# Gathered columns for eight of nine V units, own PSUM tiles for the last pair, and a new order for every engine

## The chip, the cores and the metric

The kernel runs on one core of a Trainium2 chip. The metric is the time of one execution in microseconds of the device; lower is better. Besides TensorE (PE in the profile; its weight loads are PEld), the core has VectorE (DVE), ScalarE (ACT), GpSimd (POOL) and SyncE (SP). SP does no arithmetic here: it issues DMAs in its own order, and ACT issues some too.

## The reference

One transformer block with conditioning, for 2048 positions of 448 features, in bf16:

```
mod = silu(c) @ w_mod, cut into sa, ca, ga, sb, cb, gb
h = layernorm(x) * (1 + ca) + sa
x = x + ga * (attention(h) @ wo)
h = layernorm(x) * (1 + cb) + sb
x = x + gb * (silu(h @ w1) @ w2)
```

The attention has 16 heads of 28 features. Each position looks at 8 keys: itself and the positions 2, 4, ... 14 behind it. w1 is 448 x 1792, w2 is 1792 x 448.

## The kernel before

**Layout.** Even and odd positions never meet in the attention, so each half is a sequence of 1024 positions with a plain window of 8. The kernel holds h transposed (features on partitions) in `hT`, two tiles `hA` and `hB` of 512 positions per parity. The sequence is worked in four chunks of 256 positions per parity for normalisation and projection, in nine attention units of two blocks (57 queries and 64 keys per block and parity), and in four chunks for the feed-forward part.

**Stages and the names of their operations.** A number after the name is the chunk, unit or pair.

- `ldx`, `ldm`, `ldwv`, `ldwqk`, `ldwo`, `ldw1`, `ldw2`, `ldc`: loads. `pad`: four copies that spread the QK weights into `wp` (L441).
- `n1m.*` and `n2m.*`: layer norms of 256 rows: statistics (`st` on DVE, L361 and L362, or `mean`, `sq` with ACT, L371), `rstd` on POOL (L374, L375), `nm`, `xn0`, `xn1` (L393 on ACT, L395 on DVE).
- `h0x.trp` on PE for the first chunk, or `n1m.tr`, a DMA transpose issued by SP (L412). Then `hk.mod`: scale and shift per feature, on DVE (L236) or ACT (L234).
- `qkkg.S` and `.C`: the QK projection of chunk k, head group g (L483), and `.ev`, its copy out of PSUM (L487).
- `vu.S` and `.C`: V for the keys of unit u (L517 or L518) and `.ev` (L523).
- `lgu`: logits of a unit (L555), `exu0`, `exu1`: exp on ACT (L562), `mku`: mask on DVE (L613), `avu`: attention times V on PE (L629), `rcu` and `onu`: normalise on DVE (L636, L641), `otru`: DMA transpose by SP (L644), `alu`: copies that close the gaps (L651 to L659).
- `wom.S` and `.C`: output projection of 256 rows (L686), `resm`: residual with row sums on DVE (L694).
- `gk.mod`, `f1ki.S`, `.C` (L714), `.ev` (silu on ACT, L719); `f2m.S0` to `.C2` (L741) for row pairs 0 to 6, and `f27.F0` to `.F3` (L753) for the last pair; `yam`: add the residual on DVE (L774), `stom`: store (L779, L781).

Matmuls with 64 rows of contraction come in twos on the two halves of the array: `.S` uses the half with the same number as the PSUM bank, `.C` the other one.

**V, apart or whole.** A unit's two key blocks overlap, and each block has an even and an odd half that lie in different places of `hT`. For a unit in `APART` the weights are loaded straight from there, in 64 columns for one half at a time: 28 matmuls of 64x64. For any other unit `project_v` first gathers the columns into a tile `hv` with two to four copies (`hvu`, L507) on DVE or ACT, and then takes 128 columns at a time: 14 matmuls of 64x128. Two `hv` tiles are there. Before, only unit 4 is whole.

**PSUM.** Four tiles of two banks. An operation that opens a matmul group takes a tile, and the operation that reads it last gives it back. In the last pair, all four parts (`F0`, `F1`: the even rows; `F2`, `F3`: the two halves of the columns of the odd rows) write one tile, and three adds (`ya70`, `ya71`, `ya72`) read it.

**The order.** `Plan.emit` writes the instructions in the order of the text `ORDER`: a number is an operation (in the order of `P.op` calls), the letter is its engine (p PE, a ACT, v DVE, g POOL, s SP). Each engine runs its own operations strictly in that order; a DMA issue stands in the order of the engine that issues it. A dependency becomes a semaphore wait. `junk` operations are matmuls without use if they are on PE and nothing if they are on SP.

Parts of the queues before, by name:

```
PE   ccol warm junk x6 mod1.mm h00.trp h01.trp v0.S v1.S v0.C v1.C qk03.S qk02.S qk03.C qk02.C qk01.S qk00.S qk01.C qk00.C
     qk11.S qk10.S lg0 qk10.C qk11.C qk13.S qk12.S lg1 qk13.C qk12.C v3.S av0 v3.C v2.S av1 v2.C mod2.mm ga.mm qk20.S lg2 ...
     wo0.C qk32.C v5.S av3 v5.C wo1.S ... av4 v6.S v7.S v6.C v7.C ... v8.S av5 v8.C ... f106.C av6 f104.C ... f20.S2 av7 av8 f20.C0
     ... f26.C2 read f27.F0 f27.F1 f27.F2 f27.F3
DVE  ... n12.st0 n12.st1 mod1.ev h00.mod0 h01.mod0 h01.mod1 pad0 ... ya5 ya4 flag ya6 ya70 ya71 ya72
SP   ldx0a ldx0b ldm_a1 ldx1 ldm_a0 ldwv0 ldwqk0 n13.tr n12.tr ldm_b0 ldm_c0 ldm_c1 ldm_b1 n14.tr ldwo1 n15.tr ...
     otr3 ldw1a0 n20.tr otr4 n21.tr ldw1b1 otr5 ... sto1 sto5 sto70 sto71 sto6
ACT  ldc tab silu_c scT n10.xn0 ldwv1 ... h00.mod1 ldx2 ldx3 ... f136.ev sto72
```

Of the kernel before, what the change touches and what calls it, by code (L numbers as in the profile page):

```python
# [45 lines left out]
32g 241a 16a 242a 132p 129p 193v 192v 194g 130a 133v 137p 235p 138p 134p 167s 17s 168s 172a 243v 244p 236v 237v 238s 18s 195g 169a 139a 245v 171v 170v
135p 144p 140p 136a 200g 145v 246v 201v 185v 141v 202v 203v 173p 196a 197a 253p 254a 255a 176p 146v 256v 174p 177p 186p 175a 247s 266p 178a 248v 147v
267a 187p 257p 205s 268a 204s 258v 259v 21a 179p 260s 182p 180p 206v 208v 239a 188a 209v 207v 183p 249p 216p 184v 269v 181a 279p 280a 281a 250p 251v
252v 261a 217p 218v 189p 318g 319a 20s 270p 190p 262p 213p 263p 214p 320a 321g 271v 282v 272v 191a 273s 264v 265v 283p 222p 322g 325v 225p 19s 215a
326a 327a 328g 329g 223p 226p 224a 210p 284v 323v 324v 285v 292p 227a 211p 274v 293a 294a 275p 219p 330v 331v 212a 276p 332s 295v 278v 286s 277v 401v  # L50
228p 296p 287a 229p 333s 22s 23a 230a 220p 221a 297v 298v 337v 288p 142p 403a 143a 305p 306a 307a 336v 334v 335v 289p 291v 356p 290v 308v 350p 353p
357p 402a 309p 149v 310v 358a 351p 404g 354p 352a 338p 347p 299s 300v 311v 408v 24s 154v 148v 151v 341p 409a 410a 339p 342p 348p 355a 340a 312s 301p
411g 343a 349a 150v 152v 153v 344p 302p 405g 345p 303v 304v 406v 367p 313a 346a 314p 412g 413v 414v 375p 315p 317v 316v 368p 369p 376a 377a 378v 407v
388p 389a 390a 391v 416s 359p 360p 361p 379p 392p 465g 458g 459a 466a 362p 363p 364p 467a 460a 380v 393v 381v 415s 468g 469v 470v 417a 370p 461g 394v
420v 418v 462v 419v 463a 471a 464a 371p 372p 382s 430p 424p 383a 365v 373v 427p 431p 395s 425p 432a 426a 428p 429a 421p 384p 433p 472s 473s 477a 385p
396v 387v 386v 515v 476v 434p 435a 397p 422p 436p 439p 398p 423a 475a 474a 437p 400v 399v 522v 438a 524a 490p 440p 491p 441a 442p 481p 443p 450p 451p
444p 482p 517a 516a 523a 525g 526g 527v 492a 528a 493p 518g 483a 452p 478p 519v 494p 495a 520v 521v 529s 530s 533v 366s 445p 446p 447p 496p 479p 480a
448v 453p 454p 484p 455p 556v 534a 531a 485p 487p 532a 456v 497p 488p 486a 498a 535p 538p 536p 489a 537a 539p 540a 541p 507p 508p 509p 542p 543a 449s
499p 547p 510p 511p 550p 512p 513v 500p 551p 552a 548p 544p 553p 501p 457s 549a 545p 546a 502p 554p 557p 559p 560p 555a 561p 503p 504p 505v 506s 558v
374s 514s 562p 563p 564p 567p 568p 569p 570p 571p 565v 572v 573s 574v 575s 566s 576v 577a  # L60
"""


# [78 lines left out]
def layer(ctx, tc, io, safe):  # L142

    A_x, A_wqkv, A_wo, B_w1, B_w2, c, w_mod, out = io
    nc = tc.nc
# [578 lines left out]
    def ffn2(k):  # L724
        f2_read[k] = []
        for i in range(2):
            m = 2 * k + i
            last_pair = m == 7

            cell = {}  # L730
# [15 lines left out]
                    cell["last"] = x  # L746
            mms = {}
            if last_pair:
                def full(o, par, i0, i1, c0, c1, i=i, cell=cell):
                    t = ps[cell["first"]["slot"]["ps"][0]]  # L750
                    for ii in range(i0, i1):
                        for jj in range(2):
                            matmul(t[:, par, c0:c1], lhsT=hid[:, k % 2, jj, ii, 128 * (2 * i + par):128 * (2 * i + par) + 128], rhs=w2[:, ii + 7 * jj, c0:c1],  # L753
                                   start=(ii == 0 and jj == 0), stop=(ii == 6 and jj == 1))
# [16 lines left out]
            def add(o, m=m, cell=cell, par=None, c0=0, c1=D):  # L771
                t = cell["t"] = outl if m == 7 else outb[o["slot"]["out"][0]]
                p = slice(0, 2) if par is None else slice(par, par + 1)
                V.tensor_tensor(out=t[:, p, c0:c1], in0=ps[cell["first"]["slot"]["ps"][0]][:, p, c0:c1], in1=x_all[:, 2 * m + p.start:2 * m + p.stop, c0:c1], op=ALU.add)  # L774
# [149 lines left out]
```

## Time and profile before

| | us |
|---|---|
| time, median of 3 runs | 170.31 (169.68 to 170.35) |
| the profiled execution | 169.34 |
| its span, first to last instruction | 167.5 |
| PE busy | 156.1 (93%) |
| ACT busy | 102.0 (61%) |
| DVE busy | 86.1 (51%) |
| POOL busy | 25.5 (15%) |
| mean granted clock of TensorE | 0.992 |

The profile is of one execution. The busy time of an engine is that of its instructions without waits, branches and DMA issues; a group of rows gives the source line, the engine, the operation, what it writes and reads, the shape and the count, then busy time and the mean of one, then the idle time ahead of them and what ended it. In the timeline each row is a start, a length, the engine (with q: a DMA issue), the line, the operation and the count of instructions merged. Merged matmuls are pipelined, so a row can reach past the start of the next.

### The profile page before, as it was taken

The numbers are of one execution on the slowest core, as the hardware profiler recorded it, in microseconds if no ns is written. First come the engines' busy times: TensorE is split into PE (matmuls) and PEld (weight loads), VectorE is DVE, ScalarE is ACT, GpSimd is POOL, SyncE is SP. The second block draws the span as 40 slices with busy tenths as digits, with TensorE's granted clock in tenths as the row PEclk, the third lists the DMA queues.
The fourth block names the chain that finished last, engine by engine and source line by source line (L and its number), as shares of the span: only waits on it lengthen the run. The fifth ranks groups of instructions, "written<-read, shape, count | busy, mean of one in ns | idle before, by whom it ended". The sixth has DMA issues, their size and how long they took to land. (4 is left out here: it accounts for less than half of the span.)

```text
span 167.5 us, 6069 instructions
## 1 busy us (share of the span) xinstructions
PE 156.1 (93%) x2670; PEld 80.5 (48%) x2670; DVE 86.1 (51%) x192; ACT 102.0 (61%) x138; POOL 25.5 (15%) x66
## 2 busy tenths in 40 slices
PE   2979979999999999999999999999999999999950
PEld 1254535655455555444556444454444444445540
DVE  3897899987888747692668713302152002002220
ACT  4368657879866869997976695894266620440000
POOL 7460730700002200312034000022000000000000
PEclk9999999999999999999999999999999999999996
DMA  5989978658640999920220950002411000000412
GB/s 138 348 293 242 247 289 135 180 101 171 162 126 21 198 174 293 250 56 7 59 66 22 121 125 4 0 0 57 126 55 55 4 0 4 0 0 4 170 32 87
DMA packets 33453, 18.52 MB, mean 111 GB/s; under 512 B 25102, under 2 KB 33422, under 8 KB 33422
## 3 DMA queue, kind: packets, MB, share of 16 engines
q1 hardware_dynamic: 30208, 14.46, 37.6%
q10 hardware_dynamic: 3214, 3.61, 6.9%
q8 instruction: 23, 0.38, 0.9%
q14 instruction: 8, 0.07, 0.1%
HBM read 10.21 MB, written 1.84 MB: 72 GB/s over the span
## 5 line engine op out<-in xcount | busy, mean ns | idle before, releaser
L719 ACT ACTIVATE both<-ps 128x1024 bf16<-128x1024 f32 x28 | 27.8, 1021 | 23.6 <-PE ps L714 23.6
L741 PE MATMUL ps<-w,both 64*128 64x448 bf16 x392 | 39.9, 349 | 0.0
L714 PEld LDWEIGHTS <-w 64*128 64x128 bf16 x392 | 19.0, 94 | 21.9
L741 PEld LDWEIGHTS <-both 64*128 64x128 bf16 x392 | 18.8, 94 | 18.2
L714 PE MATMUL ps<-wqk,w 64*128 64x512 bf16 x196 | 23.3, 376 | 0.0
L714 PE MATMUL ps<-h,w 64*128 64x512 bf16 x196 | 23.1, 376 | 0.0
L562 ACT ACTIVATE p<-ps 128x912 bf16<-128x912 f32 x18 | 15.8, 928 | 5.7 <-PE ps L555 5.6
L483 PEld LDWEIGHTS <-wp 64*128 64x128 bf16 x224 | 11.0, 94 | 13.4 <-issue 3.2
L694 DVE SCALAR_TENSOR_TENSOR x_all<-ps,x_all 128x448 bf16<-128x448 f32 x16 | 9.3, 621 | 15.0 <-PE ps L686 15.0
L483 PE MATMUL ps<-ha,wp 64*128 64x512 bf16 x112 | 13.2, 377 | 1.1 <-DVE ha L236 1.1
L483 PE MATMUL ps<-hb,wp 64*128 64x512 bf16 x112 | 14.0, 377 | 0.0
L487 ACT CAST qk<-ps 128x1024 bf16<-128x1024 f32 x11 | 11.0, 1016 | 4.0 <-PE ps L483 4.0
L374 POOL TENSOR_SCALAR rs<-mv 128x2 f32<-128x2 f32 x16 | 3.9, 242 | 61.3 <-ACT scr L371 45.6
L393 ACT ACTIVATE xn<-x_all,nm,rs 128x512 bf16<-128x512 bf16 x12 | 9.1, 806 | 6.2 <-DVE nm L381 5.7
L613 DVE TENSOR_TENSOR p<-p,maskb 128x1824 bf16<-128x1824 bf16 x9 | 10.1, 1118 | 4.4 <-ACT p L562 4.4
L774 DVE TENSOR_TENSOR wqk<-ps,x_all 128x896 bf16<-128x896 f32 x4 | 4.4, 1089 | 15.5 <-PE ps L741 13.4
L375 POOL TENSOR_TENSOR rs<-rs,negh 128x2 f32<-128x2 f32 x16 | 11.8, 740 | 1.3
L774 DVE TENSOR_TENSOR ot<-ps,x_all 128x896 bf16<-128x896 f32 x3 | 3.3, 1091 | 16.1 <-PE ps L741 16.1
L361 DVE BATCH_NORM_STATS2 st<-x_all 128x6 f32<-128x448 bf16 x16 | 9.7, 605 | 3.3 <-DMA x_all<-in_A_x_dram 3.3
L395 DVE TENSOR_SCALAR xn<-x_all,mv,rs 128x512 bf16<-128x512 bf16 x20 | 7.3, 402 | 6.9 <-POOL rs L375 6.5
L371 ACT ACTIVATE scr<-x_all,mv 128x448 bf16<-128x448 bf16 x16 | 10.6, 665 | 0.1
L641 DVE TENSOR_TENSOR o<-ps,rc 121x896 bf16<-121x896 f32 x9 | 9.7, 1078 | 0.2
(96 smaller groups left out, 170.8 us busy)
## 6 DMA issues: line engine op xcount, KB each, us to landing
both<-in_w_mod_dram SPq DMA_DIRECT2D x3, 672.0 KB, 6.0
w<-in_B_w_dram SPq DMA_DIRECT2D x3, 448.0 KB, 4.4
x_all<-in_A_x_dram ACTq DMA_DIRECT2D x2, 448.0 KB, 4.7
out_dram<-wqk SPq DMA_DIRECT2D x4, 224.0 KB, 2.0
w<-in_B_w_dram ACTq DMA_DIRECT2D x1, 784.0 KB, 6.1
w<-in_B_w_dram SPq DMA_DIRECT2D x1, 784.0 KB, 5.7
both<-in_w_mod_dram SPq DMA_DIRECT2D x3, 224.0 KB, 5.1
wo<-in_A_wo_dram ACTq DMA_DIRECT2D x1, 672.0 KB, 5.0
```

The lines of the kernel that those rows point to most:

```text
L361: V.bn_stats(out=st[:], in_=x_all[:, us[t], :])
L371: S.activation(out=scr[:, t, :], in_=x_all[:, us[t], :], func=ACTF.Square, bias=mv[:, t, 0:1], accum_out=mv[:, t, 1:2])
L375: G.tensor_tensor(out=rs[:], in0=rs[:], in1=negh[:], op=ALU.pow)
L483: return [matmul(t[:, j, :], lhsT=w, rhs=hT[k // 2][rows, :, kt, CP * (k % 2):CP * (k % 2) + CP], start=start, stop=stop)]
L487: copy_on(o)(out=qk[:, :, g, :, s0:s0 + CP], in_=t[:].rearrange("p j (t s) -> p j t s", t=2))
L562: S.activation(out=p_of[u][:, 2 * t * w:2 * t * w + 2 * w].rearrange("p (j n) -> p j n", j=2), in_=bank(a, t)[:, :, 0:w], func=ACTF.Exp, s ...
L613: V.tensor_tensor(out=p, in0=p, in1=m, op=ALU.mult)
L641: V.tensor_tensor(out=dims(t[0:n, :], 0, (576, 2), (DH, H), (1, DH)), in0=view(bank(a))[:, :, :, 0:DH], in1=r, op=ALU.mult)
L694: V.scalar_tensor_tensor(out=x_all[:, u, :], in0=ps[first["slot"]["ps"][0]][:, par, 0:D], scalar=1.0, in1=x_all[:, u, :], op0=ALU.mult, op ...
L714: return [matmul(t[:, i // 7, :], lhsT=w1[rows, kt, 128 * i:128 * i + 128], rhs=h[rows, :, kt, :], start=start, stop=stop)]
L719: S.activation(out=hid[:, k % 2, :, i, :], in_=t[:], func=ACTF.Silu)
L741: x = matmul(t[:, par, 0:D], lhsT=hid[half(hf), k % 2, jj, ii, 128 * j:128 * j + 128], rhs=w2[half(hf), ii + 7 * jj, :], start=(way == 0 a ...
```

## The change

- `APART` shrinks to unit 0: units 1 to 8 take gathered columns. Seven `hv` operations are added; two `hv` tiles serve them, as before.
- In the last pair `F0` and `F1` share one PSUM tile, `F2` and `F3` have one each; each add reads the tile of its part, from column 0, and gives it back.
- `ORDER` is new for every engine.

```
-APART = (0, 1, 2, 3, 5, 6, 7, 8)
+APART = (0,)
...
-                def full(o, par, i0, i1, c0, c1, i=i, cell=cell):
-                    t = ps[cell["first"]["slot"]["ps"][0]]
+                def full(o, par, i0, i1, c0, c1, i=i, mms=mms):
+                    t = ps[mms[2 * par + (c0 > 0)]["slot"]["ps"][0]][:, 0, 0:c1 - c0]
...
-                            matmul(t[:, par, c0:c1], lhsT=hid[:, k % 2, jj, ii, ...], rhs=w2[:, ii + 7 * jj, c0:c1],
+                            matmul(t, lhsT=hid[:, k % 2, jj, ii, ...], rhs=w2[:, ii + 7 * jj, c0:c1],
...
-                                  take=() if x else ("ps",), group=("F", None, 0))
+                                  take=() if x == 1 else ("ps",), group=("F", None, 0))
...
+                r = ps[(mms[2 * par + (c0 > 0)] if last_pair else cell["first"])["slot"]["ps"][0]]
+                r = r[:, p, :][:, :, c0:c1] if par is None else r[:, 0:1, 0:c1 - c0]
...
-            P.release(ad, first, "ps")
-            if not last_pair:
+            P.release(ad[:1], first, "ps")
+            if last_pair:
+                for x in (1, 2):
+                    P.release(ad[x:x + 1], mms[x + 1], "ps")
+            else:
                 P.release(st, ad[0], "out")
```

The new `ORDER`, the same stretches by name:

```
PE   ccol warm junk x8 mod1.mm h00.trp h01.trp junk x3 v0.S v0.C junk qk00.S qk03.S qk02.S qk01.S qk02.C qk03.C qk01.C qk00.C
     v1.S v1.C lg0 qk12.S qk12.C qk13.S lg1 av0 qk13.C qk10.S qk11.S qk10.C v3.S qk11.C v3.C av1 lg2 v2.S v2.C ga.mm gb.mm lg3
     ... v5.S av3 v5.C wo1.S wo0.S wo1.C lg4 wo0.C qk30.S qk32.S qk31.S av4 qk30.C qk32.C qk31.C mod2.mm ... wo2.C v8.S lg5 v8.C
     v6.S wo3.S v6.C lg6 wo3.C f102.S ... f103.C av6 av5 f20.S0 f20.S1 f20.S2 v7.S lg7 f20.C0 v7.C ... f21.S2 av7 lg8 f21.C0
     ... f114.S av8 f115.S ... f26.C2 read f27.F0 f27.F1 f27.F2 f27.F3
DVE  n10.st1 n10.st0 n11.st1 n11.st0 n12.st1 n12.st0 scT n11.nm n13.st1 n13.st0 mod1.ev h00.mod0 h01.mod1 n13.nm n13.xn0 n13.xn1
     pad3 pad1 pad0 n12.xn0 n12.xn1 (six n14 to n16 st) n14.nm n14.xn0 qk01.ev h1.mod2 h1.mod3 h1.mod0 h1.mod1 n14.xn1 n15.xn0 n15.xn1
     v1.ev mk0 ... on2 mk3 h3.mod2 wog4 w2g10 al2 ... n21.xn1 qk30.ev n20.xn0 n20.xn1 mod2.ev ... ya5 ya6 ya70 ya71 ya72
SP   ldc ldx0a ldx0b ldm_a1 ldx1 ldm_a0 ldwv1 ldwv0 ldwqk1 ldwqk0 ldx2 n13.tr n12.tr ldm_c1 ldwo0 ldm_b1 n14.tr ldwo1 n15.tr
     ldm_c0 ldm_b0 otr0 ... otr2 ldw20 ldw1a0 otr3 otr4 n21.tr n20.tr ldw1b0 ldw1a1 otr6 ... sto4 sto5 sto6 sto72
ACT  ... h00.mod1 h01.mod0 pad2 ldx3 v0.ev hv1 qk02.ev qk03.ev qk00.ev ldwo2 ex00 ex01 qk12.ev ex10 ex11 hv2 h2.mod1 qk13.ev qk11.ev
     h2.mod2 ex20 ex21 v2.ev ga.ev hv4 ex30 ex31 v4.ev hv5 al1 ... ex40 ex41 n21.sq1 n21.sq0 n20.sq0 n20.sq1 ldw1b1 ... f135.ev sto70 sto71
POOL ozero1 masks ... ones n13.rstd vone1 vone0 ozero0 n14.rstd ...
```

More of the change, by code (lines that the diff above doesn't have):

```diff
@@ L46 @@
[L46 to L57, printed above, removed]
@@ L58 @@
[L58 to L60 removed]
+32g 25a 26g 2s 58a 29g 33g 59p 0s 35p 56p 1s 69v 68v 70g 57p 38p 55s 47s 71g 4s 75v 74v 76g 9s 106v 105v 52s 3s 42s 6s 51p 48p 36p 37p 54p 60v 30g 77v
@@ new lines @@
+72a 49s 41s 112v 111v 62p 73a 80p 78a 79a 5s 8s 45s 83p 107g 108g 34g 44p 63v 81v 82a 113g 43p 85v 7s 114v 115v 116v 67v 65v 64v 40p 39s 50s 10s 46s
+118s 28g 27g 109v 110v 84a 66a 11a 98p 99p 100a 159v 158v 165v 31g 160g 117s 164v 196v 197v 161v 162v 53p 101a 86p 95p 92p 89p 93p 94a 96p 90p 91v
+121v 122v 119v 120v 166g 167g 163v 97a 87p 102p 103p 15s 16s 168v 169v 88a 238p 18a 129p 130p 239a 240a 104v 132p 241v 131a 203v 247p 248a 13s 242p
+133p 170s 17s 171s 202v 139v 123p 243v 249a 244v 198g 250v 126p 124p 14s 135a 173a 12s 140p 134a 127p 125v 128a 141p 142v 251p 260p 174a 245s 136p
@@ new lines @@
+261a 137p 175v 262a 199g 204g 205g 138a 252v 172v 61v 143p 145p 253v 246v 206v 207v 273p 144a 182p 146v 24s 200v 201v 188a 189p 274a 275a 185p 263v
+190p 191a 192a 264p 149v 265v 209s 266v 276v 183p 254s 208s 176p 186p 255a 179p 187a 184a 177p 180p 193p 267s 212v 150v 156v 277p 178a 194p 181a 195a
+210a 211a 268v 278v 213v 279v 269p 256p 270p 272v 271v 286p 257p 287a 288a 259v 258v 214p 220p 217p 332g 289v 290p 291v 292v 334a 333a 325g 326a 327a
+22a 215p 221p 218p 335g 23s 19s 280s 336v 337v 338v 147p 293s 328g 222a 223p 281a 216v 282p 329g 330v 331v 148v 219v 234a 224p 225a 283p 226v 285v
@@ new lines @@
+284v 294v 235p 299p 151v 300a 301a 236p 237v 227p 295p 340s 339s 344a 228p 229a 312p 313a 314a 408g 409a 410a 411g 296p 157v 343v 342v 341v 297v 155v
+298v 152v 154v 415v 412g 21s 20s 351p 345p 363p 357p 364p 358p 346p 352p 365a 359a 413a 347a 360p 348p 361p 353a 362a 354p 349p 350a 355p 356a 302v
+153v 315v 230v 316p 303p 317v 417a 414a 416a 418g 419v 304v 305v 318v 366p 367p 368p 231p 382p 369p 383a 384a 420v 421v 319s 385v 423s 422s 232p 320a
+233a 374p 370p 371p 372v 375p 376p 386p 395p 306s 387v 377p 378p 379p 388v 307v 426v 389s 321p 425a 424a 427a 396a 397a 380v 398v 308p 322p 323v 309p
@@ L61 @@
+546p 542p 549p 543p 506p 507p 550a 547a 560p 508p 456s 561p 562a 554p 509p 555p 551p 510p 552p 556a 553a 511p 514p 557p 544a 566p 558p 515p 516p 512v
+559a 567p 568p 517p 518p 569p 570p 519p 373s 520v 513s 521s 571p 572v 573s 574p 575p 576p 577p 578p 579v 580a 581v 582a 583v 584s
 """
@@ L770, in ffn2, with add @@
             ends = [] if last_pair else [mms[0, 2], mms[1, 2]]
-            def add(o, m=m, cell=cell, par=None, c0=0, c1=D):
+            def add(o, m=m, cell=cell, mms=mms, last_pair=last_pair, par=None, c0=0, c1=D):
                 t = cell["t"] = outl if m == 7 else outb[o["slot"]["out"][0]]
                 p = slice(0, 2) if par is None else slice(par, par + 1)
-                V.tensor_tensor(out=t[:, p, c0:c1], in0=ps[cell["first"]["slot"]["ps"][0]][:, p, c0:c1], in1=x_all[:, 2 * m + p.start:2 * m + p.stop, c0:c1], op=ALU.add)
+                r = ps[(mms[2 * par + (c0 > 0)] if last_pair else cell["first"])["slot"]["ps"][0]]
+                r = r[:, p, :][:, :, c0:c1] if par is None else r[:, 0:1, 0:c1 - c0]
+                V.tensor_tensor(out=t[:, p, c0:c1], in0=r, in1=x_all[:, 2 * m + p.start:2 * m + p.stop, c0:c1], op=ALU.add)
             def store(o, m=m, cell=cell, par=None, c0=0, c1=D):
```

10 lines of the change are left out of this document (5 added, 5 removed).

## The prediction

> **What bounds the kernel now.** I read the page first: busy shares, then the slices.
>
> ```profile
> PE 156.1 (93%) x2670; PEld 80.5 (48%) x2670; DVE 86.1 (51%) x192; ACT 102.0 (61%) x138; POOL 25.5 (15%) x66
> PE   2979979999999999999999999999999999999950
> ```
>
> TensorE is busy in every slice but the first, two near 20 us, and the last two. So the time is where its queue begins, plus the work in it, plus its waits, plus what follows its last matmul. The timeline of PE alone shows these (start, length, line, count). Lengths of merged rows overlap, so I take differences of starts.
>
> ```profile
> 8.90 0.95 PE L322 MATMUL ps<-scT,both 128*128 128x1 bf16 x32 [0.65 <-DMA both<-in_w_mod_dram]
> ...
> 14.47 6.54 PE L483 MATMUL ps<-ha,wp 64*128 64x512 bf16 x58
> 21.36 0.39 PE L483 MATMUL ps<-ha,wp 64*128 64x512 bf16 x2 [0.36 <-DVE ha L236]
> 22.45 1.47 PE L483 MATMUL ps<-ha,wp 64*128 64x512 bf16 x12 [0.70 <-DVE ha L236]
> 23.85 0.70 PE L555 MATMUL ps<-qk 28*64 28x57 bf16 x64
> 24.49 3.30 PE L483 MATMUL ps<-ha,wp 64*128 64x512 bf16 x28
> ...
> 48.81 0.95 PE L518 MATMUL ps<-wv,hb 64*64 64x448 bf16 x16
> ...
> 50.88 0.93 PE L686 MATMUL ps<-wo,oa 64*128 64x448 bf16 x8
> ...
> 67.29 3.40 PE L714 MATMUL ps<-h,w 64*128 64x512 bf16 x30
> 70.62 0.68 PE L629 MATMUL ps<-v,p 64*57 64x29 bf16 x64
> 71.23 6.00 PE L714 MATMUL ps<-h,w 64*128 64x512 bf16 x54
> 77.07 0.92 PE L686 MATMUL ps<-wo,ha 64*128 64x448 bf16 x8
> ...
> 89.26 5.47 PE L741 MATMUL ps<-w,both 64*128 64x448 bf16 x56
> 94.57 5.56 PE L714 MATMUL ps<-wqk,w 64*128 64x512 bf16 x50
> ...
> 155.75 5.51 PE L753 MATMUL ps<-w,both 128*128 128x448 bf16 x42
> ```
>
> The last matmul ends at 155.75 + 5.51 = 161.26; the span is 167.5. Prices: a 512-column matmul (77.07 - 71.23) / 54 = 0.108 us; a 448-column one on 64x128 tiles (94.57 - 89.26) / 56 = 0.0948. An av stage alone takes 71.23 - 70.62 = 0.61, and the 30 matmuls ahead of it take 3.33 where 30 x 0.108 = 3.24, so entering its tile shape costs 0.09: 0.70 in all. Logits take 24.49 - 23.85 = 0.64 plus 0.11 by the same reasoning: 0.75.
>
> **Part 1: V from gathered columns.** A whole unit is 14 matmuls x 0.0948 = 1.33. An apart unit is 28 matmuls on 64x64 tiles: unit 5 with av3 inside it takes 50.88 - 48.81 = 2.07, against 1.33 + 0.61 = 1.94 whole. So the matmuls cost the same either way, and only switches of shape go: 0.13 for unit 5, the same by likeness for unit 8. In the other units the apart V shared its switch with two matmul groups, so I take nothing there. In the new order av and logits stand side by side three times (lg1 av0, av1 lg2, av7 lg8), which saves part of an entry of 0.09: 0.1 in all. Together **-0.35 us**. The copies: eight gathers where there was one on DVE; now hv1, hv2, hv4, hv5 and hv8 are on ACT, hv3, hv6 and hv7 on DVE, mostly two copies of 512 elements. I price them, and an evacuation on ACT, with the rows of the near sizes in the groups by form.
>
> ```profile
> L487 ACT CAST qk<-ps 128x1024 bf16<-128x1024 f32 x11 | 11.0, 1016 | 4.0 <-PE ps L483 4.0
> L651 ACT COPY oa<-op 128x448 bf16<-128x448 bf16 x1 | 0.6, 564 | 0.9 <-DMA op<-o 0.9
> L507 DVE COPY hv<-ha 128x504 bf16<-128x504 bf16 x1 | 0.3, 287 | 0.0
> ```
>
> About 1.15 us on ACT and 0.57 on DVE for a unit. ACT is idle 39% of the span; the cover is that hv1, hv4, hv5 and hv8 stand many matmul groups ahead of their readers. hv2 is not covered (part 3).
>
> **Part 2: the order at the start.** PE did v0 and v1 ahead of the QK projections; the new queue does v0 alone, then eight QK halves, then v1. The rows of the way there (SP, then DVE):
>
> ```profile
> 1.70 0.43 SPq L239 DMA_DIRECT2D both<-in_w_mod_dram  x1
> ```
>
> ```profile
> 7.04 0.63 DVE L361 BATCH_NORM_STATS2 st<-x_all 128x6 f32<-128x448 bf16 x1 [0.56 <-DMA x_all<-in_A_x_dram]
> ...
> 10.05 0.13 DVE L326 COPY modc<-ps 128x4 f32<-128x4 f32 x1
> ...
> 10.36 2.00 DVE L236 TENSOR_SCALAR ha<-ps,modc 128x256 bf16<-128x256 bf16 x6
> 12.28 0.38 DVE L441 COPY wp<-wqk 128x896 bf16<-128x896 bf16 x1
> 12.58 0.73 DVE L395 TENSOR_SCALAR xn<-x_all,mv,rs 128x512 bf16<-128x512 bf16 x2
> ...
> 19.82 2.58 DVE L236 TENSOR_SCALAR ha<-ha,modc 128x512 bf16<-128x512 bf16 x3
> ...
> 44.08 1.38 DVE L236 TENSOR_SCALAR hb<-hb,modc 128x512 bf16<-128x512 bf16 x4 [0.26 <-DMA hb<-xn]
> ```
>
> ```profile
> 19.99 2.26 POOL L283 MEMSET o<- 128x1088 bf16 x2
> ```
>
> ldc moves to the head of SP's queue, so all of SP's loads issue 0.43 later: x arrives for n12's statistics at 7.04 + 0.43 = 7.47, mod1.mm starts at 8.90 + 0.43 = 9.33. DVE then does four statistics (about 0.74 each) with scT and n11.nm among them, to 10.7, where mod1.ev was at 10.05; four half-width mods (2.00 / 6 each) to 12.1; n13.nm and two xn, 0.86, to 13.0; three pads, 0.35 each, to 14.1. The QK projections need the pads, so they would start at 14.15. But one ozero memset now falls about 12.3. In the rows above, three mods took 2.58 beside two such memsets where four took 1.38 without: (2.58 - 3 x 0.35) / 2 = 0.77 for one memset. I take half of it, since the stage may fall beside DVE work that does not slow: start **14.5 (+0.03 against 14.47)**, ends 14.15 and 14.9. v1 comes after: **+1.33**. The loads ldwv1, ldwqk1 and ldx2 move from ACT into SP's queue and issue earlier; nothing waits behind them but n13.tr, which needs xn at 13.0 anyway.
>
> The wait at 20 us goes: 72 projection matmuls between 14.47 and 23.85 take 9.38 where 72 x 0.108 and 0.1 to leave make 7.88: **-1.5**. In the new order v1 stands there, and the h1 mods no longer meet the memsets.
>
> **Part 3: new waits.** From its start PE has 112 QK matmuls (12.1), v1 and v3 (2.66), two logits (1.5) and two av (1.4 - 0.1) before lg2: due 14.5 + 17.6 = 32.1. lg2 needs qk13.ev and qk11.ev, and on ACT these stand behind hv2 and h2.mod1, which needs the transposes n14.tr and n15.tr.
>
> ```profile
> 24.20 2.19 SPq L412 DMA_TRANSPOSE hb<-xn  x1
> 26.44 0.60 SPq L239 DMA_DIRECT2D wo<-in_A_wo_dram  x1
> 27.14 1.33 SPq L412 DMA_TRANSPOSE hb<-xn  x1
> ```
>
> ```profile
> 31.55 1.52 ACT L234 ACTIVATE hb<-hb,modc 128x512 bf16<-128x512 bf16 x2 [0.45 <-DMA hb<-xn]
> ```
>
> These rows say that the second transpose, issued at 27.14, let ACT go at 31.55: 4.4. Now DVE ends qk01.ev (behind PE's 50th matmul) at about 14.5 + 5.4 + 1.2 = 21.1, four mods at 22.5, n14.xn1 at 22.9, n15's two at 23.6; SP issues n14.tr, ldwo1, n15.tr at 22.9, 24.2 to 25.1, 24.9 to 25.8. h2.mod1 starts at 29.3 to 30.2, takes 0.76 and is followed by two casts of 1.0: lg2 at 32.0 to 33.0. **+0.5**, ends 0 and 1.6 (both transposes at 2.19 and a longer landing). At f102.S, PE needs g0's mods and ldw1a1, the second load that SP issues after n20.tr: **+0.2**. For al2 before wo1.S and one late PSUM tile **+0.2**. Elsewhere I followed the evacuations against PE's running sum and found each PSUM tile free 0.3 to 2 us ahead.
>
> PE's end: 161.26 + 0.03 + 1.33 - 1.5 - 0.35 + 0.9 = 161.67, **+0.4**.
>
> **Part 4: three tiles and the tail.**
>
> ```profile
> 161.36 1.22 DVE L774 TENSOR_TENSOR qk<-ps,x_all 128x448 bf16<-128x448 f32 x3 [3.80 <-PEq L891]
> 162.01 1.17 SPq L781 DMA_DIRECT2D out_dram<-qk  x2
> 162.61 0.38 ACTq L781 DMA_DIRECT2D out_dram<-qk  x1
> 163.24 0.42 SPq L779 DMA_DIRECT2D out_dram<-wqk  x1
> ```
>
> The three adds share a PSUM tile with all four matmul parts and start 0.1 after the last of them, though the first half was complete 2.8 us earlier. sto6 issues last, at 163.24, and the span ends 4.26 later. With own tiles only ya72 is left behind the last matmul: 0.1 + 0.38 (a half add, 1.22 less 0.62, with overlap), issue 0.03 later, and sto6 stands ahead of it on SP. End = PE's end + 0.51 + 4.26 = +4.77, where it is +6.24: **-1.5**, ends -0.6 and -1.9 (a 56 KB store may land sooner than the 224 KB one).
>
> **Sum:** +0.4 - 1.5 = -1.1. The profiled execution took 169.34 (span 167.5 and 1.84 around it), 0.97 under the median of 170.31. I set the difference against the median: **169.2 us**. A measurement here can tell about 0.5%, 0.85 us, from no change.
>
> **Rivals.**
> 1. The early waits stay away: transposes land for lg2 in time, and PE starts at 14.15: -0.9 and -0.35, so 168.0. For it: 0.5 of my waits leans on one landing. Against it: ACT's idle 0.45 at 31.55 was that same landing.
> 2. Three tiles do not part the adds (DVE waits for PE's last count): the adds end 1.3 behind PE, only sto6's place is gained, -0.6 in place of -1.5: 170.1. The 3.80 wait is put down to PE's sequencer, which fits both.
> 3. Slower: w1 comes late. Both ldw1b0 and ldw1a1 stand on SP behind otr4, n21.tr and n20.tr. The row for their like (size, and time to landing):
>
> ```profile
> w<-in_B_w_dram SPq DMA_DIRECT2D x3, 448.0 KB, 4.4
> ```
>
> By my sum n20.xn1 ends near 57.8, ldw1a1 issues at 60.0 and lands 4.4 later, at 64.4, or up to 1.3 after that by an estimate, since its neighbour's 448 KB go ahead of it; f102's third step needs it at 65.5. Each us later is a us lost: past 66.6 the gain is gone, past 67.5 it is slower by over 0.5%. n20's chain (two squares on ACT behind ex41, POOL, nm, xn behind qk30.ev) need only be 2.5 us late; then 171.4. Against it: ACT's share leaves room.
> 4. The memset at 12.3 blocks the pads whole: a 1.16 us stop (2.26 / 2 and a gap) instead of 0.35 at PE's start, +0.8: 170.0. [...] The trace shows 0.77 for one memset, between the two.
>
> **Chances.** Forecast 0.35, rival 1 0.22, rival 2 0.13, rival 3 0.20, rival 4 0.10. Forecast 0.25 faster, 0.10 same; rival 1 faster; rival 2 same but 0.01; rival 3 0.15 slower, 0.05 same; rival 4 0.03 faster, 0.07 same. Sum: faster 0.51, same 0.34, slower 0.15. The range reaches from below rival 1 (-0.6 for the better end of the tail and the spread of runs) to near rival 3: 167.4 to 171.1; the forecast alone 168.5 to 169.9.
>
> **What would show it.** PE's QK projections from 14.2 to 14.9; no wait of 1.5 near 21; lg2 not before 32; the first add near PE's end less 2.7, and the last store 0.5 after PE's end. Wrong if PE waits over 1 us at f102.S or anywhere behind it, or if the adds still start together.

## The result, and the profile after

| | before | after |
|---|---|---|
| median, us | 170.63 (20 runs) | 174.22 (20 runs, 171.26 to 178.38) |
| ratio | | 1.0116 [1.0071, 1.0162] |
| the profiled execution | 169.34 | 174.29 |
| its span | 167.5 | 172.6 |
| last matmul ends | 161.26 | 168.20 |
| span behind it | 6.24 | 4.4 |

The change made the kernel slower by 1.2%, about 2.0 us, where the prediction said 169.2 us (167.4 to 171.1). The ratio leaves out the longer executions of both kernels, among them the one of 174.29 us that was profiled, so a cost that its profile shows counts here only as far as after_again's profile (173.38 us, below) shows it too. The page of the changed kernel, shares, TensorE's slices and the granted clock:

```profile
PE 159.5 (92%) x2584; PEld 80.1 (46%) x2584; DVE 89.2 (52%) x200; ACT 100.7 (58%) x140; POOL 24.9 (14%) x66
PE   4969999996986999999999999999999999999990
PEclk9987999999999999999999999999999999999999
```

PE is busy for 159.5 us, 3.4 longer than before with 86 matmuls fewer; there are holes near 41 and 53 us (the tenth and the thirteenth slice) where the kernel before has none, and only the last slice is empty, where before the last two were half and wholly so. The timeline of PE at these places (start, length, line, count, the wait ahead):

```profile
10.51 0.95 PE L322 MATMUL ps<-scT,both 128*128 128x1 bf16 x32 [1.72 <-DVE nm L381]
...
14.01 1.63 PE L518 MATMUL ps<-wv,ha 64*64 64x448 bf16 x16
15.81 0.76 PE L518 MATMUL ps<-wv,ha 64*64 64x448 bf16 x12 [0.17 <-PEq L217]
...
16.73 6.21 PE L483 MATMUL ps<-ha,wp 64*128 64x512 bf16 x56
...
34.42 0.68 PE L629 MATMUL ps<-v,p 64*57 64x29 bf16 x64
35.03 0.70 PE L555 MATMUL ps<-qk 28*64 28x57 bf16 x64
35.68 0.93 PE L517 MATMUL ps<-wv,hv 64*128 64x448 bf16 x8
36.76 0.74 PE L517 MATMUL ps<-wv,hv 64*128 64x448 bf16 x6 [0.15 <-PEq L217]
...
39.05 0.21 PE L555 MATMUL ps<-qk 28*64 28x57 bf16 x2
40.86 0.69 PE L555 MATMUL ps<-qk 28*64 28x57 bf16 x62 [1.59 <-issue]
...
50.77 0.56 PE L629 MATMUL ps<-v,p 64*57 64x29 bf16 x49
53.36 0.29 PE L629 MATMUL ps<-v,p 64*57 64x29 bf16 x15 [2.03 <-issue]
...
162.70 5.50 PE L753 MATMUL ps<-w,both 128*128 128x448 bf16 x42
```

Three things are new. The QK projections begin at 16.73 (14.47 before). Between the two halves of one V unit or QK pair stands a wait for PE's own sequencer where nothing else lies between them: v1, qk12 and v2 each take 0.32 to 0.34 more than their matmuls. And PE stops in the middle of lg3 and of av3, 2 and 49 matmuls into a stage, for 1.59 and 2.03 us, with nothing named that it waits for ("issue"). Behind 53.36 no row of PE waits over 0.1 us.

The tail, DVE's adds and the stores:

```profile
165.56 0.62 DVE L776 TENSOR_TENSOR qk<-ps,x_all 128x448 bf16<-128x448 f32 x1 [1.60 <-PE ps L753]
166.22 1.54 ACTq L783 DMA_DIRECT2D out_dram<-qk  x2
166.97 0.39 DVE L776 TENSOR_TENSOR qk<-ps,x_all 128x224 bf16<-128x224 f32 x1 [0.79 <-PE ps L753]
168.25 0.39 DVE L776 TENSOR_TENSOR qk<-ps,x_all 128x224 bf16<-128x224 f32 x1 [0.88 <-PE ps L753]
168.66 0.34 SPq L783 DMA_DIRECT2D out_dram<-qk  x1
```

Each add now starts behind its own part; one half add and one store are left behind the last matmul, and the span ends 4.4 behind it: 1.84 less than before.

PE's end follows from these: 161.26, + 2.26 (start), + 1.33 (v1 behind the projections), - 1.5 (the wait at 20 us, gone), + 0.98 (three pairs of halves), + 3.80 (stops of 1.59, 2.03 and one of 0.18 inside av2) = 168.13; measured 168.20.

### The profile page after: what moved, and what is told of

Same layout as the page of the kernel before. It is cut to its first block, busy times and chain, and to the rows that moved or that the text cites. A ratio compares the mean times of both kernels' runs of the same rounds, so it can differ in the third digit from the quotient of the medians.

```text
span 172.6 us, 5892 instructions
## 1 busy us (share of the span) xinstructions
PE 159.5 (92%) x2584; PEld 80.1 (46%) x2584; DVE 89.2 (52%) x200; ACT 100.7 (58%) x140; POOL 24.9 (14%) x66
## 3 DMA queue, kind: packets, MB, share of 16 engines
q1 hardware_dynamic: 32510, 16.93, 40.6%
HBM read 10.21 MB, written 1.84 MB: 70 GB/s over the span
## 4 chain that ended last, share of the span: by engine, by line
PE 89%; DMA 4%; issue 3%; DVE 1%; SPq 1%; PEldq 0%
PE ps L714 25%; PE ps L741 22%; PE ps L483 15%; PE ps L517 7%; PE ps L686 6%; DMA x_all<-in_A_x_dram 4%; PE ps L555 3%; PE ps L629 3%; PE ps L753 3%; PE ps L518 1%; PE ps L322 1%; PE ps L297 1%; SPq L239 1%; PE ps L340 1%; PE ps L455 1%
## 5 line engine op out<-in xcount | busy, mean ns | idle before, releaser
L741 PE MATMUL ps<-w,both 64*128 64x448 bf16 x392 | 39.2, 349 | 0.0
L776 DVE TENSOR_TENSOR ot<-ps,x_all 128x896 bf16<-128x896 f32 x5 | 5.5, 1092 | 32.1 <-ACT both L719 19.4
L714 PE MATMUL ps<-h,w 64*128 64x512 bf16 x196 | 21.5, 376 | 0.0
L483 PEld LDWEIGHTS <-wp 64*128 64x128 bf16 x224 | 10.3, 94 | 12.3 <-PEq L217 0.6
L487 ACT CAST qk<-ps 128x1024 bf16<-128x1024 f32 x12 | 11.6, 1016 | 4.9 <-PE ps L483 4.9
L517 PE MATMUL ps<-wv,hv 64*128 64x448 bf16 x112 | 13.1, 350 | 0.3 <-PEq L217 0.3
L483 PE MATMUL ps<-hb,wp 64*128 64x512 bf16 x112 | 13.3, 377 | 0.0
L636 DVE RECIPROCAL rc<-ps 121x32 f32<-121x32 f32 x9 | 3.2, 356 | 14.2 <-PE ps L629 14.2
L395 DVE TENSOR_SCALAR xn<-x_all,mv,rs 128x512 bf16<-128x512 bf16 x25 | 9.7, 430 | 0.6 <-POOL rs L375 0.6
L374 POOL TENSOR_SCALAR rs<-mv 128x2 f32<-128x2 f32 x16 | 3.4, 213 | 43.7 <-ACT scr L371 28.3
```

Of the source, the lines that this page charges most:

```text
L483: return [matmul(t[:, j, :], lhsT=w, rhs=hT[k // 2][rows, :, kt, CP * (k % 2):CP * (k % 2) + CP], start=start, stop=stop)]
L487: copy_on(o)(out=qk[:, :, g, :, s0:s0 + CP], in_=t[:].rearrange("p j (t s) -> p j t s", t=2))
L517: return [matmul(t[:, j, 0:D], lhsT=w, rhs=wv[rows, kt, :], start=start, stop=stop)]
L714: return [matmul(t[:, i // 7, :], lhsT=w1[rows, kt, 128 * i:128 * i + 128], rhs=h[rows, :, kt, :], start=start, stop=stop)]
L741: x = matmul(t[:, par, 0:D], lhsT=hid[half(hf), k % 2, jj, ii, 128 * j:128 * j + 128], rhs=w2[half(hf), ii + 7 * jj, :], start=(way == 0 a ...
```

## The experiments

Their edits are moves in the order of one queue, written with the operations' names. Ratios are to the kernel before on the same chip, five rounds each unless said.

### The change once more, and its parts

**after_again** is the changed kernel, for comparison.

> The changed kernel, unchanged, for an execution to read beside the first profile (span 172.6). Theory: three costs outweigh a tail that is 1.84 us shorter: the start (the QK projections began at 16.73 where 14.47 was), halves of one matmul pair back to back (0.32 us each, four places), and stops inside matmul groups at every 256th instruction of TensorE's program (1.59, 0.18 and 2.03 us). The stops should differ from execution to execution while the other two stay: here 0 to 4 us of stops, again at multiples of 256 instructions, and QK projections again at 16 to 17. Rival: the stops are fixed to places in the program and come with the same length again.

173.53 us, ratio 1.0106 [1.0024, 1.0188]. Its profile has the stop in lg3 again (1.72 us) and, behind it, qk22.S and v4.S at half speed; the stop in av3 did not come again.

```profile
40.75 0.69 PE L555 MATMUL ps<-qk 28*64 28x57 bf16 x62 [1.72 <-issue]
41.37 1.89 PE L483 MATMUL ps<-hb,wp 64*128 64x512 bf16 x8
43.05 1.70 PE L517 MATMUL ps<-wv,hv 64*128 64x448 bf16 x8
```

From qk22.S to av2 this takes 46.18 - 41.37 = 4.81, where the first profile has 44.64 - 41.48 = 3.16: 1.65 more. The projections began at 16.12, so the same sum gives 161.26 + 1.65 (start) + 1.33 - 1.5 + 0.98 + 1.72 + 1.65 = 167.09 for PE's end; measured 167.17. The start, the halves and the stop in lg3 thus stand in both profiles; the 2.03 in av3 is one execution's alone.

**before_tail**: the kernel before with the change's tail alone.

```diff
-APART = (0,)
+APART = (0, 1, 2, 3, 5, 6, 7, 8)
 # ORDER: the kernel before's, but
-  f26.C2 ... ya6 ya70 ya71 ya72;  SP: sto70 sto71 sto6;  ACT: sto72
+  f26.C2 ya6 sto6 ... ya70 ya71 ya72;  SP: sto6 sto72;  ACT: sto70 sto71
```

> The kernel before with the last part of the change alone: three PSUM tiles for the last pair, sto6 ahead of the last stores on SyncE, sto70 and sto71 on ScalarE, sto72 on SyncE. Theory: from the last matmul to the end of the span 4.4 us where 6.24 was, so about 168.7 of 170.5 (ratio 0.989), PE's queue as before. Rival: the three tiles bring something late to the last matmuls (a tile not free for the third part), and the gain is under 0.5 us.

168.06 us, ratio 0.9864 [0.9816, 0.9912], and once more on another chip, as **tail_again**:

> The same kernel as before_tail (old order, V as before, three tiles and the new stores for the last pair), for comparison on this chip with spread. Again 0.982 to 0.991 of the kernel before. If spread is at the same ratio within 0.5%, the new order of TensorE with the gathered columns is worth nothing by itself, and all that the change brings is its tail; if spread is lower by 0.5% or more, the order brings something once its loads are out of the way of the code.

168.40 us, 0.9895 [0.9862, 0.9929]. The timeline of before_tail:

```profile
156.29 5.51 PE L753 MATMUL ps<-w,both 128*128 128x448 bf16 x42
...
162.25 0.34 SPq L783 DMA_DIRECT2D out_dram<-qk  x1
```

PE ends at 161.80 and the span at 166.3, 4.5 behind it (6.24 before). The tail is a gain of 1.1 to 1.4%, and this version is faster than both kernels.

**vwhole**: the same with V units 5 to 8 from gathered columns.

```diff
-APART = (0, 1, 2, 3, 5, 6, 7, 8)
+APART = (0, 1, 2, 3)
 # ACT: hv5 behind ex30, hv8 behind v6.ev;  DVE: hv6 behind res01, hv7 behind on3
-SP: sto6 sto72;  ACT: sto70 sto71
+SP: sto6 sto70 sto71;  ACT: sto72
```

> The old order with the three tiles for the last pair (the version that gave 168.1), and V units 5 to 8 from gathered columns too: hv5 and hv8 on ACT, hv6 and hv7 on DVE, nothing else moved. Theory of the prediction: 14 matmuls of 64x128 cost what 28 of 64x64 cost, only the switches of shape at units 5 and 8 go: -0.26 us, 167.8; the copies are hidden. Rival 1: the unit with whole rows is slower than that, since its two halves stand closer and wait (0.32 each): 168.4 or more. Rival 2: the copies delay evacuations on ACT or DVE and PE waits behind them: 168.6 or more.

169.67 us, 0.9921 [0.9867, 0.9975]: no gain over the tail alone, and rather a loss, though the intervals overlap. One thing more was moved than the expectation says: the engines of the last three stores are swapped. The span still ends 4.4 us behind PE's end (162.03), as in the tail alone (4.5), so this does not explain a loss.

```profile
43.43 2.34 PE L483 MATMUL ps<-hb,wp 64*128 64x512 bf16 x20 [0.68 <-ACT p L562]
...
49.18 0.92 PE L517 MATMUL ps<-wv,hv 64*128 64x448 bf16 x8
50.03 0.38 PE L629 MATMUL ps<-v,p 64*57 64x29 bf16 x25
50.58 0.47 PE L629 MATMUL ps<-v,p 64*57 64x29 bf16 x39 [0.17 <-issue]
50.98 0.74 PE L517 MATMUL ps<-wv,hv 64*128 64x448 bf16 x6
51.55 0.92 PE L686 MATMUL ps<-wo,oa 64*128 64x448 bf16 x8
```

Unit 5 with av3 takes 51.55 - 49.18 = 2.37, of which 0.34 is a stop inside av3 (0.95 where an av takes 0.61); 2.03 without it, against 2.06 apart. So the switch was worth 0.03, not 0.13. And hv5 on ACT ahead of ex31 makes the QK projection wait 0.68 for its PSUM tile: rival 2.

### The start, and the halves

**loads**: the changed kernel with four loads back on ACT.

```diff
-SP:  ldc ldx0a ldx0b ldm_a1 ldx1 ldm_a0 ldwv1 ldwv0 ldwqk1 ldwqk0 ldx2 n13.tr
+SP:  ldx0a ldx0b ldm_a1 ldx1 ldm_a0 ldwv0 ldwqk0 n13.tr
-ACT: tab silu_c n10.xn0 n10.xn1 n11.xn0 n11.xn1 h00.mod1
+ACT: ldc tab silu_c n10.xn0 ldwv1 n10.xn1 n11.xn0 ldwqk1 n11.xn1 h00.mod1 ldx2
```

> The changed kernel with four loads issued by ScalarE again, at the places they had before: ldc first, ldwv1 behind n10.xn0, ldwqk1 behind n11.xn0, ldx2 behind h00.mod1. Theory: x of the second chunk arrives at 7.1 to 7.5 where 8.75 was, so the statistics ahead of scT end earlier, mod1.mm starts near 9.2 where 10.51 was, and the QK projections at 15.4 where 16.73 was: 1 to 1.5 us faster than the changed kernel on this chip. Rival: the loads share the same DMA engines wherever they are issued, x arrives as late as before, and the time is the same within 0.5 us.

172.71 us, 1.0106 [1.0021, 1.0191]. The projections start at 14.05, 2.7 earlier than in the changed kernel's profile, and the ratio stays where after_again's was:

```profile
39.06 0.69 PE L555 MATMUL ps<-qk 28*64 28x57 bf16 x62 [2.06 <-issue]
39.68 1.08 PE L483 MATMUL ps<-hb,wp 64*128 64x512 bf16 x8
40.55 1.70 PE L517 MATMUL ps<-wv,hv 64*128 64x448 bf16 x8
42.04 1.92 PE L483 MATMUL ps<-hb,wp 64*128 64x512 bf16 x8
```

lg3 stops for 2.06, and then 8 matmuls take 1.49 (40.55 to 42.04) where the price is 8 x 0.0948 = 0.76, and the next 8 take 1.70 (42.04 to 43.74) in place of 0.86. So the stop and what follows it cost 2.06 + 0.73 + 0.84 = 3.6.

**cross**: other work between the halves.

```diff
-PE: v1.S v1.C lg0 qk12.S qk12.C qk13.S ...  v2.S v2.C ga.mm
+PE: v1.S lg0 v1.C qk12.S qk13.S qk12.C ...  v2.S ga.mm v2.C
```

> The changed kernel with another matmul group put between the two halves of three pairs: lg0 between v1.S and v1.C, qk13.S between qk12.S and qk12.C, ga.mm between v2.S and v2.C. Theory: the second half waits for the end of the first, and with nothing between them this takes 0.32 us each (1.08 where 0.76 is the length of v1.S): 1.0 us faster than the changed kernel, and the rows of the three pairs lose their waits for TensorE's own sequencer. Rival: those waits lie in time that the next group would have waited anyway (for its evacuations), and under 0.4 us is gained.

174.00 us, 1.0191 [1.0120, 1.0262]: no gain. The sequencer's waits are gone and others stand in their places:

```profile
23.38 0.70 PE L555 MATMUL ps<-qk 28*64 28x57 bf16 x64 [0.35 <-ACT qk L487]
...
28.50 0.67 PE L629 MATMUL ps<-v,p 64*57 64x29 bf16 x64 [0.56 <-ACT qk L487]
...
36.61 0.93 PE L340 MATMUL ps<-both,screp 128*128 128x448 bf16 x4 [0.22 <-DVE screp L310]
```

What was brought forward was not ready. The 0.98 of the halves is a price of this order as a whole.

### The stop inside a stage

If all instructions that the trace has on TensorE's own queues are counted (matmuls, weight loads and a few for semaphores), lg3 stops at the 1218th instruction in the changed kernel, after_again, loads and cross (1.59, 1.72, 2.06, 1.42 us); av2 at the 1474th, av3 at the 1730th: 256 apart. The trace has, on queue q8, DMA records of 16384 bytes of the kind "instruction" (22 of them, 0.36 MB, in the changed kernel), which is 64 bytes for each of 256. By these two, TensorE's program comes in blocks of 256. The DMA view of the changed kernel, first from 34.60, when PE enters the block of instructions 962 to 1217, to 38.3, then the 1.3 us behind that (the last figure is the time of the packets as a share of 16 engines):

```profile
DMA packets 2044, 1.20 MB, mean 325 GB/s; under 512 B 1072, under 2 KB 2044, under 8 KB 2044
q1 hardware_dynamic: 2044, 1.20, 116.2%
```

```profile
DMA packets 19, 0.02 MB, mean 14 GB/s; under 512 B 16, under 2 KB 18, under 8 KB 18
q8 instruction: 1, 0.02, 5.2%
q1 hardware_dynamic: 18, 0.00, 1.1%
```

For 3.7 us the loads fill the queues and no instruction packet moves; when they are through, the fetch begins at 38.39, and PE goes on 2.47 later. The theory: the next block is fetched while the one before it runs, but the fetch waits behind the loads in the queues. The rival: av1 and lg2 side by side simply use 256 instructions too fast.

**early21**: ldw21 (784 KB) out of the way.

```diff
-SP: ldm_b1 n14.tr ldwo1 n15.tr ldm_c0 ldm_b0 otr0 ldw21
+SP: ldm_b1 ldw21 n14.tr ldwo1 n15.tr ldm_c0 ldm_b0 otr0
```

> The changed kernel with one transfer moved: ldw21 (784 KB of w2) stands ahead of n14.tr on SP, to issue near 19.5 us, where it issues at 32 to 33 us. Theory (code): TensorE stops at its 1218th instruction, inside lg3, because the 16 KB of instructions from there on are fetched only when ldw21's packets have drained (fetch starts at 38.39, 38.19, 36.55 and 38.51 us in four profiles, each time with the last of these packets). Then the fetch starts 2.5 us or more ahead of lg3, the stop of 1.4 to 2.1 us goes, and the half clock behind it in three of four profiles goes too: the profile shows no issue stop over 0.5 us near index 1218, qk22.S 0.86 and v4.S 0.76, and the time is 1.5 to 3.5 us less than the changed kernel's 174: 170.5 to 172.5. Rival (rate): av1 and lg2 side by side use 256 instructions in 1.3 us, faster than the fetch can follow whatever the DMA engines do: the stop stays at 1.4 us or more and the time at 173.5 to 174.5. Second rival: the early load only shifts the trouble, n14.tr lands later and lg2 waits, or the stop comes one block of 256 instructions earlier near 27 us: 173 to 175.

171.99 us, 1.0027 [0.9963, 1.0091]: the time that the theory gave, but the stop is only cut, to 0.98, and the half clock behind it is gone (qk22.S's row is 1.04 long, after_again's 1.89). The fetch began at 37.25, when ldm_c0, ldm_b0 (672 KB each) and all but the last 0.25 us of the transposes were through.

**swap**: these two ahead as well.

```diff
-SP: ldm_b1 n14.tr ldwo1 n15.tr ldm_c0 ldm_b0 otr0 ldw21
+SP: ldm_b1 ldm_c0 ldm_b0 n14.tr ldwo1 n15.tr ldw21 otr0
```

> The changed kernel with three transfers in other places of SP's queue: ldm_c0 and ldm_b0 (672 KB each) ahead of n14.tr, and ldw21 (784 KB) behind n15.tr where those two stood. In early21 the fetch of TensorE's next 16 KB of instructions still began only at 37.25 us, when ldm_c0, ldm_b0 and the transposes had drained, and TensorE stopped 0.98 us at its 1218th instruction. Theory (code behind loads): the fetch waits for the drain of whatever stands in the DMA queues; here some 34 us at the latest. So the fetch starts 2.5 us or more ahead of lg3, no issue stop there, and the time is 0.9 to 1.2 less than early21's, 1.5 to 3.5 less than the changed kernel's: 169.8 to 171.3. Rival (rate): the fetch comes late because av1 and lg2 use 256 instructions in 1.3 us; it starts again within 2 us of lg3 and the stop is 0.9 or more. Second rival: four w_mod loads ahead of n14.tr make this transpose land late and lg2 waits over 0.5: 171 to 172.

170.67 us, 1.0026 [0.9979, 1.0074].

```profile
26.21 0.26 PE L629 MATMUL ps<-v,p 64*57 64x29 bf16 x11
27.39 0.58 PE L629 MATMUL ps<-v,p 64*57 64x29 bf16 x53 [0.92 <-issue]
27.91 3.20 PE L483 MATMUL ps<-ha,wp 64*128 64x512 bf16 x28
...
33.01 0.68 PE L629 MATMUL ps<-v,p 64*57 64x29 bf16 x64
33.61 0.70 PE L555 MATMUL ps<-qk 28*64 28x57 bf16 x64
...
37.64 0.83 PE L555 MATMUL ps<-qk 28*64 28x57 bf16 x64
```

lg3 (37.64) runs through, though av1 and lg2 (33.01, 33.61) stand side by side as before: the rival falls. (Not all of the gain in this profile is the stop's: its projections began at 14.33, where early21's began at 16.03.) The stop is now inside av0, at instruction 706, two blocks earlier: that fetch came only at 24.77, in the traffic of the four w_mod loads. The stop moved with the loads.

**before_load** makes the stop in the old order.

```diff
-SP: otr0 ldwo2 otr1;  ldw20 on ACT and ldw21 on SP, both later
+SP: otr0 ldwo2 ldw21 ldw20 otr1
```

> The kernel before with two loads of w2 (ldw21 and ldw20, 784 KB each) moved up to stand behind ldwo2 on SP, to issue near 35 us. The old order, the old tail, V as it was: only the DMA queues are fuller between 35 and 40 us. Theory (code behind loads): the fetch of the 16 KB from instruction 1474 on, at 36.6 us in the kernel before and 3.8 us ahead of its use, begins only when these packets have drained, near 39 to 40; TensorE stops at instruction 1474 (about 40.5 us) with an issue stop of 1 to 2.5 us that the kernel before does not have. Rival (rate, or the new order itself): no issue stop, the fetch starts by 37.5. Both expect other waits from the transposes that now queue behind these loads, so the total time (171 to 175) tells nothing.

175.42 us in its one run. (This kernel's lines stand one lower.)

```profile
42.77 3.19 PE L482 MATMUL ps<-hb,wp 64*128 64x512 bf16 x27
47.26 0.37 PE L482 MATMUL ps<-hb,wp 64*128 64x512 bf16 x1 [1.30 <-issue]
```

The stop is there, 1.30 us, in a QK projection of the old order: one block later than expected (instruction 1730), since SP issued the two loads at 36.6 to 37.8, when the fetch for 1474 (37.81) was starting. The fetch for 1730 began at 44.48, 3.4 after its block was entered; in the kernel before it was 1.25.

**mended**, **loadswap** and **spread** tried to have both, the early start and no stop. They were, in this order: early21's move and loads' moves, with scT ahead of n12's statistics on DVE and the memset ozero0 behind n14.rstd on POOL; swap's and loads' moves; and loadswap with ldwo2 moved from ACT to SP behind n15.tr, and ldw21 behind otr0.

> The changed kernel with ldw21 moved as in early21, the four loads ldc, ldwv1, ldwqk1 and ldx2 back on ACT as in the kernel before, the scT cast ahead of n12's statistics on DVE, and the ozero0 memset behind n14.rstd on POOL. Theory: the start (QK projections at 16.7 us where the kernel before has 14.5) and the code stop with its half clock are two separate losses of 2.3 to 2.9 and 1.5 to 3.5 us: here the QK projections start at 13.3 to 14.0, nothing stops at lg3, PE ends near 162, and the time is 174 - 2.6 - 2.8 = 168.6, range 167.5 to 169.8, about that of the tail alone on the old order (168.1). Rival: the new order has a third loss of its size elsewhere (the halves back to back, 0.32 each, or new waits once the two are gone): over 170.5.

> As swap, and ldc, ldwv1, ldwqk1 and ldx2 back on ACT as in the kernel before (with nothing else of mended). Theory: the two losses are separate and both go: QK projections at 13.9 us as in loads, no stop and no half clock at lg3; loads' profile had a span of 169.9 with 2.26 + 1.6 lost there, so a span of 166 and a time of 168 to 169.5. Rival 1: an earlier start only meets later waits (lg0 or av0 for evacuations and masks, lg2 for the transposes), as in mended: over 170.5. Rival 2: the stop stays: over 171.5.

> The changed kernel with its loads spread: as loadswap (ldc, ldwv1, ldwqk1 and ldx2 on ACT; ldm_c0 and ldm_b0 ahead of n14.tr), and ldwo2 (672 KB) moved from ACT near 20.6 us to SP behind n15.tr, ldw21 behind otr0. Order of TensorE, V and the tail are the changed kernel's. Theory (code behind loads): swap and loadswap stopped at instruction 706 (0.92 and 1.64 us) because the fetch for it began only when the w_mod loads and ldwo2 had drained, near 25 to 26 us; with 672 KB less in the queues it begins by 24, 3 us ahead of its use. No issue stop over 0.3 us anywhere, QK projections at 14.0 to 14.8, span 165.3 to 166.5, time 167.3 to 169.0, a ratio to the kernel before of 0.98 to 0.99. Rival: the loads that moved hold up the next fetch instead (instruction 962 near 32 us or 1218 near 37 us), stop of 0.5 to 2 us with the half clock behind it: 169.5 to 172.

mended 172.69, 1.0120 [1.0070, 1.0171]; loadswap 169.40 to 173.35 in six runs, median 172.72, without a ratio (kernel before there: 170.76); spread 172.17, 1.0075 [1.0036, 1.0113]. All three expectations fell. In mended the stop in lg3 is gone (one of 0.40 stands in av0), and PE waits elsewhere, first for a copy that stands on DVE behind n14's statistics, which waited 3.03 us for x, and then 0.92 ahead of av1 for one on ACT:

```profile
23.99 0.70 PE L555 MATMUL ps<-qk 28*64 28x57 bf16 x64 [1.80 <-DVE qk L487]
```

In loadswap and spread the stop in av0 is 1.64 and 1.81, with half clock behind it. The row behind the stop in loadswap:

```profile
29.31 3.17 PE L483 MATMUL ps<-ha,wp 64*128 64x512 bf16 x14
```

Fourteen matmuls take 3.17 here; swap's row at 27.91 has 28 in 3.20, and in spread 28 take 4.44. In spread the fetch for 706 began at 27.11, 3.5 after its block was entered, in spite of 672 KB less ahead of it: the transposes and w_mod loads issued later there (first w_mod load at 19.94, swap 16.24), so the traffic met the same block again.

The fetches side by side, from the DMA records and the timelines (us; "after" is the changed kernel):

```
kernel       next block   entry into the   fetch    packet   PE at the    stop
             begins at    block before it  begins    took    next block
after           706           24.78         25.59     0.99      28.69      none
before         1730           40.46         41.71     1.08      44.72      none
swap           1218           33.18         34.32     1.08      37.64      none
cross           962           28.58         31.24     0.93      34.38      none
after          1218           34.60         38.39     1.08      40.86      1.59
after_again    1218           34.11         38.19     1.12      40.75      1.72
loads          1218           32.13         36.55     1.12      39.06      2.06
cross          1218           34.38         38.51     1.11      40.85      1.42
early21        1218           33.90         37.25     1.19      39.89      0.98
swap            706           22.39         24.77     1.11      27.39      0.92
loadswap        706           22.81         26.27     1.20      28.70      1.64
spread          706           23.62         27.11     1.40      29.81      1.81
mended          706           24.24         26.55     1.23      29.20      0.40
before_load    1730           41.11         44.48     1.11      47.28      1.30
after          1474           40.86         43.02     0.96      45.26      0.18
before_tail     962           27.73         29.27     2.16      32.63      0.41
after          1730           45.26         49.97     1.89      53.36      2.03
```

In all stops of this table but the last two, the fetch begins 2.2 to 4.4 us behind the entry, and from its beginning to the next block's first instruction stand 2.2 to 2.8 us. A late fetch alone is no stop: in cross it was 2.66 late for block 962, but the block before took 5.8 us to run, and there was time left. The last two rows are of another kind, for there the packet itself took 2.16 and 1.89. And the last one, the stop in av3, does not fit the theory: from 45.3, right behind the entry, to 48.0 the queues held no load and no transpose (the one packet is another queue's instructions), and the fetch still began only at 49.97.

```profile
DMA packets 1, 0.01 MB, mean 3 GB/s; under 512 B 0, under 2 KB 0, under 8 KB 0
```

So the theory is shown for the stops that moved with the loads; what held up av3's fetch stays open.

## Why the prediction was wrong

Right were the wait at 20 us (gone, 1.5), v1's 1.33, and the tail: the first add was said to start 2.7 ahead of PE's end (2.64 measured), the last store 0.5 behind it (0.46), the gain to be 1.5 (1.84, and 1.74 in before_tail by 6.24 - 4.5). Rival 2 (the adds not parted) and rival 3 (w1 late) did not come: PE does not wait at f102.S. Rival 4 neither: the three pads took 0.99, and the memset, 13.31 to 14.33, fell on n13's two xn, which took 1.33 in place of 0.73. Part 3's new waits, +0.9, were not there: lg2 started at 35.03, right behind av1, and in loads, whose start was 14.05, at 32.56 just so. That much of rival 1 came true.

Wrong by its own steps:

1. **Part 2, "start 14.5 (+0.03)".** Measured 16.73, which is 2.23 later. Half of it lies ahead of mod1.mm. x for n12's statistics was forecast 0.43 later, at 7.47; it came at 8.78, for its load, issued at 2.61 in place of 2.18, needed 6.2 us in place of 4.9. scT stands behind these statistics on DVE, and mod1.mm, forecast at 9.33, began at 10.51, 1.18 late:

```profile
8.78 0.63 DVE L361 BATCH_NORM_STATS2 st<-x_all 128x6 f32<-128x448 bf16 x1 [1.95 <-DMA x_all<-in_A_x_dram]
...
10.28 0.13 DVE L308 CAST scT<-ps 128x4 bf16<-128x4 f32 x1
...
13.46 1.33 DVE L395 TENSOR_SCALAR xn<-x_all,mv,rs 128x512 bf16<-128x512 bf16 x2
```

   Counting one issue slot of 0.43 was the error: "nothing waits behind them" was said of the moved loads, but their bytes went into the queue that carries x, q1 (16.93 MB, 14.46 before); in loads, with them back on ACT (q1 15.78), x came at 7.08. (In after_again, cross, early21 and swap mod1.mm waited for w_mod's load, to 9.42 to 10.06.) The other half lies behind mod1.mm, where the prediction followed DVE to the pads and took PE's clock as full. PE worked from mod1.mm to the QK projections with one wait of 0.17, for 6.22 us where the forecast has 14.5 - 9.33 = 5.17, at a mean granted clock of 0.73; the pads had ended at 15.70, 1.03 earlier. The stretch in this profile, and in swap's, which is at full clock (from and to, length, busy time of PE, PEld, DVE, ACT and POOL, granted clock, DMA share, GB/s):

```profile
10.51:16.73 6.22, 6.05 (x84) 3.03 (x86) 6.04 (x18) 4.37 (x8) 3.18 (x10) 0.73 0.77 272
9.42:14.33 4.91, 4.71 (x85) 2.63 (x86) 4.60 (x16) 3.81 (x7) 2.92 (x9) 1.00 0.90 326
```

   In the fourteen profiles this stretch takes 4.83 to 5.60 us at full clock (eight of them) and 6.06 to 6.41 at 0.72 or 0.73 (after, after_again, cross and early21, but of the old order tail_again and before_load too). So the start scatters: with the loads on SP the projections began at 14.33 to 16.73, with them on ACT at 14.05 to 15.57, in the old order at 14.44 to 16.59. The medians differ by about 1.5 (16.06, 14.54, 14.51), those of mod1.mm by less (9.97, 9.56, 8.91). How much of the start the moved loads cost is thus not settled.
2. **A term that is missing: halves back to back.** 0.98, from three rows. The kernel before shows none, since other work lies between its halves; that was to be read from the list of PE's queue.
3. **A term that is missing: code behind loads.** 3.80 in this execution, 1.72 with 1.65 of half clock behind it in after_again. The prediction took SP's loads as free when their readers came late, and named their queue only. swap and before_load show the mechanism for the stop in lg3 (1.59 and 1.72) by moving loads alone; why the packets of code stand behind those of data isn't shown, and the 2.03 in av3 has no cause that the runs show.
4. **Part 1, -0.35.** The one switch that was measured alone was worth 0.03, and the copies weren't free (0.68 behind ACT in vwhole). Both are readings of the old order; in the new one the term was not measured by itself.

So the likeliest case had its gain at the end, and lost that and about 2 us more ahead of 57 us. What the new order is worth by itself stays open: no run has it without a stop. swap's span of 167.0 less its stop of 0.92 is 166.1, where before_tail has 166.3 (and 0.41 of a stop of its own; one execution each), so the order and the gathered columns seem worth nothing measurable. The best version measured is before_tail.

## What to carry to other kernels

Loads that nobody waited for had a price here all the same, stops of 0.40 to 2.06 us, where they stood in the queues while TensorE ran through a block of 256 instructions in 4.1 to 5.1 us: look in the profile for stops inside a stage without a releaser, count the instructions, and see when the fetch began. Where bulk loads can stand without such a stop was not found here: spread took 672 KB out of the way and stopped for 1.81. Change the tail by itself first: it was worth more than all else here, and it was hidden behind an order that lost more than that.
